# Writing a group's exponentials earlier in the instruction order of a fused convolution and two-layer MLP kernel

## The chip, the core and the metric

The kernel runs on one core of a Trainium2 chip. The core has engines that work side by side, each through its own queue in strict order: TensorE (PE in the profile; its weight loads are PEld), VectorE (DVE), ScalarE (ACT), GpSimd (POOL) and SyncE (SP), which starts the DMA transfers here. The metric is device time in microseconds (us); lower is better.

## The reference, cut to what matters

```python
w = np.exp(weight_gen - max(weight_gen)) ; w = w / (sum(w) + 1e-9)   # softmax over 7 taps
...
out = np.einsum('bshk,bskhg->bshg', w, x_unf)     # causal convolution, own weights at each position
...
rms = np.sqrt(np.mean(x * x) + 1e-6) ; xn = x / rms * rms_g          # layer 1
g = xn @ w_gate ; val = xn @ w_val ; x = (silu(g) * val) @ w_out     # 192 -> 1536 -> 192
...
h = x @ w_in ; out = (h * sigmoid(1.702 * h)) @ w_out                # layer 2: 192 -> 2048 -> 192
```

There are 8192 tokens of 192 channels; each position has 8 heads of 7 taps. All of it is float32.

## The kernel before, in words

The tokens are cut into 16 blocks of 512. Each block b goes through these steps:

- **Softmax weights**, for a group of blocks at once (GROUPS: block 0, block 1, blocks 2-3, then 4-6, 7-9, 10-12, 13-15). VectorE takes maxima (L175) and subtracts (L178): the part called pre. ScalarE takes the exponentials in one instruction (L185): ex. VectorE sums (L188), adds 1e-9 and inverts (L191, L192) and multiplies (L195): post. The tile is wraw.
- **Convolution** (conv_ops) on VectorE: seven multiplications (L226, into acc or xr) and six additions (L259), then the squares for the rms on ScalarE (L269), the power -1/2 on GpSimd (L274, L276) and the scaling (L280). A transposition and DMAs turn the block, and ScalarE and VectorE split it into a high and a low part (L319 xh, xsh; L320 xl, xsl).
- **Layer 1** in 12 units (1, b, m). TensorE forms pg and pv in PSUM, ScalarE takes silu of pg (L460, p), VectorE multiplies by pv (L464, p), ScalarE casts (L465, h), VectorE takes the remainder (L468, l). Two units later TensorE multiplies h and l by the output weights, into a and b.
- **Y**: the sums a and b of layer 1 become the input of layer 2 (L512 to L518; yh, yl, ysh, ysl).
- **Layer 2** in 8 units (2, b, i), each with two tiles ph, silu written twice by ScalarE (L481 h, L482 p) and two remainders on VectorE (L488 l), which TensorE needs one or two units later. **Z** (L530 to L538) writes the block out.

The PSUM tiles pg, pv and ph share four buffers, so a unit can start only when the tiles of two units before have been read. A pair of matmuls on the two row halves is issued together. When a PSUM bank passes from one half to the other, TensorE waits for a word that GpSimd passes on (L390); these words stand in GpSimd's queue in program order.

The units are written in the order 4 units of block b+1 (m = 0 to 3), 8 units of layer 2 of block b, then units 4 to 11 of layer 1 of block b+1, and so on. Work on the convolution of the next block is woven in: add_work(1, end, ops) puts operations in a stream that has to be written by unit end, share sets an even pace until then, and some writes an operation whenever credit allows. The convolution of block nxt is woven in from unit (1, nxt-2, 4) on (for block 4 from (1, 2, 10)), and has to be written by unit (2, nxt-2, 6), two units ahead of xt_at[nxt], where the block is turned. For a block that opens a group (nxt = 4, 7, 10, 13), pre has to be written by unit ex_at, ex is written there, and only then do post and the convolution enter the stream, with what is left of the same time:

```python
ex_at = i + 4 if gi == 2 else pos[2, nxt - 2, 2]
add_work(1, ex_at, pr)
...
if ex_hook and i == ex_at:
    ex_hook()
    ex_hook = None
    add_work(1, xt_at[nxt] - 2, post_ops + conv_ops(nxt))
```

So these exponentials stand behind the second layer-2 unit of blocks 2, 5, 8 and 11, and the stream behind them has four units, (2, nxt-2, 2) to (2, nxt-2, 5).

Of the kernel before, what the change touches and what calls it, by code (L numbers as in the profile page):

```python
# [41 lines left out]
def gated_conv_mlp(ctx: ExitStack, tc: tile.TileContext, xp, wg, w1, wo1, w2, wo2, g, out):  # L42
# [111 lines left out]
    def softmax_load(gi):  # L154
        b0, b1 = GROUPS[gi]
        n = sum(BLOCKS[b0:b1])
        t = smw.tile([P, n * 56], F32, tag="wraw", name=f"wraw{gi}")
        nc.sync.dma_start(out=t, in_=wg[:, T0[b0] * 56:(T0[b0] + n) * 56])
        return t
# [45 lines left out]
    def load_x(*bs):  # L205
        T = sum(BLOCKS[b] for b in bs)
        t0 = T0[bs[0]]
        t = big.tile([P, (T + HALO) * D], F32, tag="x", name=f"x{bs[0]}")
        cuts = [0] + [T0[b] + BLOCKS[b] + HALO - t0 for b in bs]
        for c0, c1 in zip(cuts, cuts[1:]):  # L210
            nc.sync.dma_start(out=t[:, c0 * D:c1 * D], in_=xp[:, (t0 + c0) * D:(t0 + c1) * D])
        for b in bs:
            xch[b] = t[:, (T0[b] - t0) * D:]
# [82 lines left out]
    def shuffle_x(b):  # L296

        T = BLOCKS[b]
        N = T * P
        xr = xrow.pop(b)  # L300
        h, l, sh, sl = (xtp.tile([P, NM], F32R, tag=tag, name=f"{tag}{b}") for tag in ("xh", "xl", "xsh", "xsl"))
        xT[b] = (h, l, sh, sl)
        raw = squares[0].tile([P, T * D], F32, tag="raw", name=f"raw{b}")
        nc.vector.transpose(out=raw.rearrange("p (c j t) -> p j c t", j=T, t=Q),
                            in_=xr[:, :, 0:D].rearrange("p j (c t) -> p j c t", t=Q))
        raw = raw.rearrange("p (c n) -> p c n", n=T * Q)
        full = P // Q
        for q in range(full):
            rows = slice(q * Q, (q + 1) * Q)
            cols = slice(q * T * Q, (q + 1) * T * Q)  # L310
            for c in range(D // Q):
                dst = l if c < full else sl
                for at in ((c,) if c < full else (c - full, c - full + 2)):
                    nc.sync.dma_start(out=dst.bitcast(F32)[at * Q:(at + 1) * Q, cols], in_=raw[rows, c])

        def split():
            for c, (h_, l_) in enumerate(((h, l), (sh, sl))):
                v = l_.bitcast(F32)[:, :N]
                nc.scalar.activation(out=h_[:, :N], in_=v, func=AF.Identity, scale=gt[:, c:c + 1])  # L319
                nc.vector.scalar_tensor_tensor(out=l_[:, :N], in0=v, scalar=gt[:, c:c + 1],  # L320
                                               in1=h_[:, :N].bitcast(F32), op0=ALU.mult, op1=ALU.subtract)
        return split
# [106 lines left out]
    def matmuls(ups, downs, soon=False):  # L429

        ds = [down_halves(*d) for d in downs]
        if not ups:
            (ah, al), (bh, bl) = downs_of(ds, 0, UPPER, True), downs_of(ds, 1, UPPER, False)
            (Bh, Bl), (Ah, Al) = downs_of(ds, 1, LOWER, True), downs_of(ds, 0, LOWER, False)
            upper, lower = ah + al + bh + bl, Bh + Bl + Ah + Al
        elif len(ds) < 2 or soon:
            ua, ub, lb, la = up_halves(*ups)(True)
            (ah, al), (bh, bl) = downs_of(ds, 0, UPPER, True), downs_of(ds, 1, UPPER, False)
            (Bh, Bl), (Ah, Al) = downs_of(ds, 1, LOWER, True), downs_of(ds, 0, LOWER, False)
            upper = ua + ah + al + ub + bh + bl  # L440
            lower = lb + Bh + (la + Bl if len(ds) > 1 else Bl + la) + Ah + Al
        else:
            ua, ub, lb, la = up_halves(*ups)(False)
            (ah, al), (bh, bl) = downs_of(ds, 0, UPPER, False), downs_of(ds, 1, UPPER, True)
            (Bh, Bl), (Ah, Al) = downs_of(ds, 1, LOWER, False), downs_of(ds, 0, LOWER, True)
            upper, lower = ub + bh + ua + bl + ah + al, la + Ah + Al + lb + Bh + Bl
        for f, g in zip(upper, lower, strict=True):
            f()
            g()
# [104 lines left out]
    pos = {u: i for i, u in enumerate(units)}  # L554
# [48 lines left out]
    def add_work(k, end, ops):  # L603
        streams[k].extend((end, c, f) for c, f in ops)

    def run_work(upto):
        for q in streams:
            while q and q[0][0] <= upto:
                q.popleft()[2]()

    def share(k, i):

        total, rate = 0.0, 0.0
        for end, c, _ in streams[k]:
            total += c
            rate = max(rate, total / max(1.0, at[min(end, len(units))] - at[i]))
        return rate * (at[i + 1] - at[i])

    def some(amounts):
        for k, a in enumerate(amounts):  # L620
            credit[k] += a
        while True:
            ready = [k for k in (0, 1) if streams[k] and credit[k] > 0]
            if not ready:
                return
            for k in ready:
                q = streams[k]
                spent = 0.0
                while q and credit[k] > 0 and spent < 1500:
                    _, c, f = q.popleft()  # L630
                    f()
                    credit[k] -= c
                    spent += c
# [3 lines left out]
    with ExitStack() as order:  # L637
# [42 lines left out]
        nxt = 1  # L680
        ex_hook = None
        start_at = None
        for i, u in enumerate(units):
            kind, b, m = u
            if (kind, b, m) == (1, 2, 0):
                early.close()
                late = ctx.enter_context(tc.tile_pool(name="late", bufs=6))
                parts.append((late, late))
                squares.append(ctx.enter_context(tc.tile_pool(name="squares", bufs=1)))
            run_work(i)  # L690
            late = [splits.pop(i)] if i in splits else []
            if i in xt_by_pos:
                if 2 < nxt < NB - 1:
                    load_x(nxt + 1)
                if nxt > 3:
                    splits[pos[1, nxt - 1, M1 - 2]] = shuffle_x(nxt)
                else:
                    split = transpose_x(nxt, nxt > 2)
                    late += [split] if nxt > 1 else []
                    if nxt == 1:  # L700
                        split()
                nxt += 1
                if nxt == 2:
                    start_at = pos[1, 1, 1]
                elif nxt < NB:
                    start_at = i
            if i == start_at:
                if nxt < 4:
                    load_x(nxt)
                end = xt_at[nxt]  # L710
                gi = group_of.get(nxt)
                if gi is not None and gi >= 2:
                    pr, ex_hook, post_ops = softmax_ops(gi, sm[gi])
                    ex_at = i + 4 if gi == 2 else pos[2, nxt - 2, 2]
                    add_work(1, ex_at, pr)
                else:
                    add_work(1, end - 2, conv_ops(nxt))
                gi = group_of.get(nxt + 1)
                if gi is not None and gi >= 2:
                    sm[gi] = softmax_load(gi)  # L720
# [4 lines that stand above are left out]
            downs, after = [], []  # L725
            while pend and pend[0][0] <= i:
                _, D_, key = pend.popleft()
                d, f = D_(*key)
                downs.append(d)
                after += [f] if f else []  # L730
            second, third = (U1 if kind == 1 else U2)(b, m, lambda *ups: matmuls(ups, downs, kind == 2 and b < 2))
            todo = [share(k, i) / 2 for k in (0, 1)]
            some(todo)
            second()
            some(todo)
            third()
            for f in late + after:
                f()
            if kind == 1:
                pend.append((i + 2, D1, (b, m)))  # L740
            else:

                last = len(units) - 1
                pend.append((i + 2 if b > 1 and m == 0 else i + 1, D2, (b, 2 * m)))
                pend.append((i + 1 if b < 2 or i + 1 == last else i + 2, D2, (b, 2 * m + 1)))
# [55 lines left out]
```

## Time and profile before

| | |
|---|---|
| time, median of 3 runs | 1274.84 us (1274.59 to 1278.19) |
| the profiled execution | 1278.1 us, span 1276.3 us |
| granted TensorE clock, mean | 0.991 |
| busy share: PE, DVE, ACT, POOL | 96%, 61%, 51%, 3% |

The span runs from the first to the last instruction in the trace. The busy shares are means over stages; a clock of 1 means 2.4 GHz, 0.5 means 1.2 GHz.

### The profile page before, as it was taken

To read this page: it belongs to the slowest core of one execution; us is meant where nothing else is said; L and a number is where in the kernel's file an instruction comes from. 1 tells how busy PE (TensorE), PEld (TensorE's weight loads), DVE (VectorE), ACT (ScalarE), POOL (GpSimd) and SP (SyncE) were. 2 spreads that over 40 slices of the span, in tenths; PEclk is the share of its full clock that TensorE was granted. 3 is DMA by queue.
4 is the path that set the end of the run, shared out by engine and by line. 5 is a ranking of instruction groups with operands and counts; after the bars stand their busy time and mean duration, and the time that the engine had idled before them with its cause. 6 is when DMAs were issued, how large, how long until landed. Compare 5 with 4: busy or idle time off the path is not lost.

```text
span 1276.3 us, 26762 instructions
## 1 busy us (share of the span) xinstructions
PE 1227.6 (96%) x10308; PEld 1149.5 (90%) x10308; DVE 782.8 (61%) x1294; ACT 652.7 (51%) x1273; POOL 32.4 (3%) x53
## 2 busy tenths in 40 slices
PE   6898999989999999999999999999998999999998
PEld 3676899979999887999999989998997999999997
DVE  8888957575646457574755666465467746545432
ACT  3565764554555545454454544546464454544553
POOL 4000000000000000000000000000000000000000
PEclk8899999999999999999999999999999999999999
DMA  5755511000101110110101010010001011000000
GB/s 195 232 178 160 161 38 69 2 32 16 46 9 34 33 30 1 44 41 13 37 32 30 1 41 22 32 41 32 18 14 36 26 32 30 1 13 18 2 14 13
DMA packets 35391, 58.03 MB, mean 45 GB/s; under 512 B 8256, under 2 KB 20928, under 8 KB 35264
## 3 DMA queue, kind: packets, MB, share of 16 engines
q1 hardware_dynamic: 35264, 56.33, 14.3%
q8 instruction: 81, 1.33, 0.4%
q14 instruction: 46, 0.38, 0.1%
HBM read 43.71 MB, written 6.29 MB: 39 GB/s over the span
## 4 chain that ended last, share of the span: by engine, by line
PE 83%; DVE 10%; ACT 4%; issue 3%; DMA 0%; POOL 0%; POOLq 0%; DVEq 0%
PE a L375 22%; PE ph L375 18%; PE pg L375 15%; PE b L375 14%; PE pv L375 14%; DVE xr L226 2%; DVE l L488 1%; DVE l L468 1%; DVE p L464 1%; DVE dec_a L104 1%; DVE acc L259 1%; ACT h L481 1%; DVE dec_s L108 1%; DVE dec_s L98 1%; ACT p L482 1%
## 5 line engine op out<-in xcount | busy, mean ns | idle before, releaser
L375 PE MATMUL a<-h,o 64*128 64x512 f32 x1792 | 520.9, 393 | 0.4 <-POOLq L390 0.2
L375 PEld LDWEIGHTS a<-h,o 64*128 64x128 f32 x1792 | 329.5, 185 | 9.0 <-POOLq L390 1.1
L375 PE MATMUL a<-l,o 64*128 64x512 f32 x896 | 313.6, 394 | 10.1 <-DVE l L488 9.9
L375 PE MATMUL b<-h,o 64*128 64x512 f32 x896 | 311.2, 393 | 8.0 <-POOLq L390 8.0
L375 PE MATMUL b<-l,o 64*128 64x512 f32 x896 | 311.6, 393 | 0.3 <-DVE l L468 0.3
L488 DVE TENSOR_TENSOR l<-p,h 128x512 fp32r<-128x512 f32 x256 | 175.8, 689 | 197.8 <-ACT p L482 196.6
L481 ACT ACTIVATE h<-ph 128x512 fp32r<-128x512 f32 x256 | 153.6, 600 | 226.8 <-PE ph L375 222.3
L375 PE MATMUL pv<-xh,w 64*128 64x512 f32 x768 | 242.6, 395 | 6.9 <-DVE p L464 6.6
L375 PE MATMUL pg<-xh,w 64*128 64x512 f32 x768 | 243.6, 395 | 1.3 <-ACT w L119 1.3
L375 PE MATMUL ph<-yh,w 64*128 64x512 f32 x1024 | 240.8, 393 | 0.0
L465 ACT CAST h<-p 128x512 fp32r<-128x512 f32 x192 | 119.2, 621 | 180.4 <-DVE p L464 180.4
L460 ACT ACTIVATE p<-pg 128x512 f32<-128x512 f32 x192 | 114.5, 597 | 182.0 <-PE pg L375 160.1
L464 DVE TENSOR_TENSOR p<-p,pv 128x512 f32<-128x512 f32 x192 | 131.5, 685 | 122.9 <-PE a L375 101.7
L468 DVE TENSOR_TENSOR l<-p,h 128x512 fp32r<-128x512 f32 x192 | 132.6, 691 | 97.1 <-ACT h L465 97.1
L375 PEld LDWEIGHTS a<-l,o 64*128 64x128 f32 x896 | 165.8, 185 | 20.4 <-DVE l L488 15.1
L375 PEld LDWEIGHTS b<-h,o 64*128 64x128 f32 x896 | 164.5, 185 | 14.3 <-POOLq L390 9.7
L375 PEld LDWEIGHTS b<-l,o 64*128 64x128 f32 x896 | 165.7, 185 | 5.0 <-DVE l L468 0.7
L375 PEld LDWEIGHTS ph<-yh,w 64*128 64x128 f32 x1024 | 149.6, 185 | 9.8 <-POOLq L390 0.2
L375 PE MATMUL ph<-yl,w 64*128 64x512 f32 x512 | 156.7, 392 | 0.0
L375 PEld LDWEIGHTS pv<-xh,w 64*128 64x128 f32 x768 | 141.0, 185 | 15.1 <-DVE p L464 9.6
L482 ACT ACTIVATE p<-ph 128x512 f32<-128x512 f32 x256 | 153.1, 598 | 0.9 <-DVE l L488 0.9
L375 PE MATMUL pv<-xl,w 64*128 64x512 f32 x384 | 150.5, 392 | 0.0
(106 smaller groups left out, 2114.6 us busy)
## 6 DMA issues: line engine op xcount, KB each, us to landing
x<-in_xp SPq DMA_DIRECT2D x15, 960.0 KB, 4.7
st<-in_w SPq DMA_DIRECT2D x20, 384.0 KB, 3.9
zt<-in_w SPq DMA_DIRECT2D x20, 384.0 KB, 3.5
st<-in_wo SPq DMA_DIRECT2D x14, 384.0 KB, 4.1
zt<-in_wo SPq DMA_DIRECT2D x14, 384.0 KB, 3.4
out_z<-za SPq DMA_DIRECT2D x16, 256.0 KB, 2.2
xl<-raw SPq DMA_DIRECT2D x192, 16.0 KB, 1.8
xsl<-raw SPq DMA_DIRECT2D x192, 16.0 KB, 1.8
```

The source lines that it names most:

```text
L98: nc.vector.tensor_scalar(out=t["s"], in0=hi, scalar1=-0x80000000, scalar2=4, op0=ALU.bitwise_and, op1=ALU.bitwise_or)
L104: nc.vector.scalar_tensor_tensor(out=ai, in0=ai, scalar=3, in1=t["s"], op0=ALU.logical_shift_left, op1=ALU.bitwise_or)
L108: nc.vector.tensor_single_scalar(t["s"], t["a"].bitcast(I32), -0x800000, op=ALU.bitwise_and)
L226: eng.tensor_tensor(out=dst.rearrange("p (q g) -> p q g", g=GRP), in0=x[:, (k + j0) * D:(k + j1) * D].rearrange("p (q g) -> p q g", g=GRP) ...
L375: ins = nc.tensor.matmul(ps[:, :N], w[rows], x[rows, :N], start=start, stop=stop)
L460: nc.scalar.activation(out=p[:, :N], in_=pg[:, :N], func=AF.Silu)
L464: nc.vector.tensor_tensor(out=p[:, :N], in0=p[:, :N], in1=pv[:, :N], op=ALU.mult)
L465: nc.scalar.copy(h[:, :N], p[:, :N])
L468: nc.vector.tensor_tensor(out=l[:, :N], in0=p[:, :N], in1=h[:, :N].bitcast(F32), op=ALU.subtract)
L481: nc.scalar.activation(out=h[:, :N], in_=ps[j][:, :N], func=AF.Silu, scale=SIG)
L482: nc.scalar.activation(out=p[:, :N], in_=ps[j][:, :N], func=AF.Silu, scale=SIG)
L488: nc.vector.tensor_tensor(out=l[:, :N], in0=p[:, :N], in1=h[:, :N].bitcast(F32), op=ALU.subtract)
```

## The change

The four groups that open at blocks 4, 7, 10 and 13 get the rule that the group of blocks 2-3 has already.

```diff
@@ -711,7 +711,7 @@
                 if gi is not None and gi >= 2:
                     pr, ex_hook, post_ops = softmax_ops(gi, sm[gi])
-                    ex_at = i + 4 if gi == 2 else pos[2, nxt - 2, 2]
+                    ex_at = i + 4
                     add_work(1, ex_at, pr)
```

The exponentials then stand ahead of unit (1, 5, 8) where they stood ahead of (2, 5, 2), 10 units earlier (likewise in blocks 8 and 11); in block 2 they move from (2, 2, 2) to (1, 3, 2), 4 units earlier.

ScalarE's queue around the exponentials of the group of blocks 7 to 9, before; in p_5_4 and the like the numbers are block and hidden tile, and the last number is a running one:

```order
L481 ACTIVATE h_5_3_6894<-ph_3_6853 128x512
L482 ACTIVATE p_5_3_6893<-ph_3_6853 128x512
L185 ACT_TABLE_LOAD
L185 ACTIVATE wraw_5184<-wraw_5184 128x672
L481 ACT_TABLE_LOAD
L481 ACTIVATE h_5_4_6963<-ph_4_6908 128x512
L482 ACTIVATE p_5_4_6962<-ph_4_6908 128x512
```

The same place in the change:

```order
L460 ACTIVATE p_5_7_6436<-pg_7_6400 128x512
L465 CAST h_5_7_6437<-p_5_7_6436 128x512
L185 ACT_TABLE_LOAD
L185 ACTIVATE wraw_5184<-wraw_5184 128x672
L460 ACT_TABLE_LOAD
L460 ACTIVATE p_5_8_6486<-pg_8_6450 128x512
L465 CAST h_5_8_6487<-p_5_8_6486 128x512
```

The two table loads and the exponentials have moved from between two layer-2 units to between the cast of unit (1, 5, 7) and the silu of unit (1, 5, 8).

VectorE's queue in layer 2 of block 5, from the remainder of hidden tile 5 on, before (acc and xr are the convolution of block 7):

```order
L488 TENSOR_TENSOR l_5_5_6969<-p_5_5_6967,h_5_5_6968 128x512
L259 TENSOR_TENSOR acc_6903<-acc_6903,xr_6902 128x768
L226 TENSOR_TENSOR xr_6902<-x_6210,wraw_5184 128x768
L259 TENSOR_TENSOR acc_6903<-acc_6903,xr_6902 128x768
L488 TENSOR_TENSOR l_5_6_7032<-p_5_6_7030,h_5_6_7031 128x512
L226 TENSOR_TENSOR xr_6902<-x_6210,wraw_5184 128x768
L259 TENSOR_TENSOR acc_6903<-acc_6903,xr_6902 128x768
L488 TENSOR_TENSOR l_5_7_7037<-p_5_7_7035,h_5_7_7036 128x512
L226 TENSOR_TENSOR xr_6902<-x_6210,wraw_5184 128x768
L259 TENSOR_TENSOR acc_6903<-acc_6903,xr_6902 128x768
L226 TENSOR_TENSOR xr_6902<-x_6210,wraw_5184 128x768
L488 TENSOR_TENSOR l_5_8_7095<-p_5_8_7093,h_5_8_7094 128x512
```

Layer 2 of block 5 in the change, from its first remainder on:

```order
L488 TENSOR_TENSOR l_5_0_6863<-p_5_0_6861,h_5_0_6862 128x512
L488 TENSOR_TENSOR l_5_1_6868<-p_5_1_6866,h_5_1_6867 128x512
L259 TENSOR_TENSOR acc_6447<-acc_6447,xr_6446 128x768
L488 TENSOR_TENSOR l_5_2_6912<-p_5_2_6910,h_5_2_6911 128x512
L226 TENSOR_TENSOR xr_6446<-x_6210,wraw_5184 128x768
L488 TENSOR_TENSOR l_5_3_6917<-p_5_3_6915,h_5_3_6916 128x512
L259 TENSOR_TENSOR acc_6447<-acc_6447,xr_6446 128x768
L488 TENSOR_TENSOR l_5_4_6982<-p_5_4_6980,h_5_4_6981 128x512
L226 TENSOR_TENSOR xr_6446<-x_6210,wraw_5184 128x768
L488 TENSOR_TENSOR l_5_5_6987<-p_5_5_6985,h_5_5_6986 128x512
L488 TENSOR_TENSOR l_5_6_7042<-p_5_6_7040,h_5_6_7041 128x512
L259 TENSOR_TENSOR acc_6447<-acc_6447,xr_6446 128x768
```

Between two remainders l there mostly stood two or three convolution operations, and now there is one at most; six operations of the convolution are left for layer 2, where all 13 stood.

VectorE's queue right behind the exponentials, in the change (wraw and mx are post's operations, acc the first multiplication of the convolution):

```order
L464 TENSOR_TENSOR p_5_8_6486<-p_5_8_6486,pv_8_6451 128x512
L191 TENSOR_SCALAR mx_6250<-mx_6250 128x64
L192 RECIPROCAL mx_6250<-mx_6250 128x64
L468 TENSOR_TENSOR l_5_8_6488<-p_5_8_6486,h_5_8_6487 128x512
L195 TENSOR_TENSOR wraw_5184<-wraw_5184,mx_6250 128x448
L464 TENSOR_TENSOR p_5_9_6532<-p_5_9_6532,pv_9_6497 128x512
L188 TENSOR_REDUCE mx_6250<-wraw_5184 128x32
L191 TENSOR_SCALAR mx_6250<-mx_6250 128x32
L192 RECIPROCAL mx_6250<-mx_6250 128x32
L468 TENSOR_TENSOR l_5_9_6534<-p_5_9_6532,h_5_9_6533 128x512
L195 TENSOR_TENSOR wraw_5184<-wraw_5184,mx_6250 128x224
L226 TENSOR_TENSOR acc_6447<-x_6210,wraw_5184 128x768
```

In the change post lies among the products p and remainders l of layer 1; one operation of it, the sum L188 of the first part, stands ahead of the first of these rows. Behind them follow p and l of unit 10, the split of the next block (xl, xsl), a multiplication of the convolution and p of unit 11. In block 2 the exponentials stand behind the four ScalarE operations of Y and ahead of the silu of unit (1, 3, 2).

## Rows read from the trace of the kernel before

**Rows 1.** The page's first line.

```profile
span 1276.3 us, 26762 instructions
```

**Rows 2.** Windows from Y to Z of blocks 2, 3, 5, 8 and 11.

```profile
core 0: us, PE busy (x) PEld busy (x) DVE busy (x) ACT busy (x) POOL busy (x), PEclk, DMA share, GB/s
248.24:305.07 56.83, 52.97 (x424) 47.13 (x423) 37.38 (x58) 29.55 (x56) 1.20 (x2) 0.94 0.07 21
330.60:379.65 49.05, 49.05 (x425) 47.35 (x424) 26.62 (x40) 25.53 (x53) 1.20 (x2) 1.00 0.08 24
479.45:533.67 54.22, 50.25 (x425) 43.89 (x424) 37.39 (x58) 29.47 (x56) 1.20 (x2) 1.00 0.07 22
708.15:762.49 54.34, 50.24 (x425) 47.38 (x423) 37.41 (x58) 29.51 (x57) 1.20 (x2) 1.00 0.07 23
936.87:991.04 54.17, 50.16 (x424) 47.45 (x423) 37.40 (x58) 29.49 (x56) 1.20 (x2) 1.00 0.08 23
```

**Rows 3.** ScalarE's timeline, block 5: start, duration, instruction, [idle before it].

```profile
492.54 1.28 ACT L185 ACT_TABLE_LOAD   x1
493.83 0.77 ACT L185 ACTIVATE wraw<-wraw 128x672 f32<-128x672 f32 x1
...
495.91 0.60 ACT L481 ACTIVATE h<-ph 128x512 fp32r<-128x512 f32 x1
```

**Rows 4.** TensorE's timeline: two waits of block 5, the last of block 2.

```profile
504.32 0.50 PE L375 MATMUL a<-l,o 64*128 64x512 f32 x1 [1.13 <-DVE l L488]
...
515.49 0.49 PE L375 MATMUL b<-h,o 64*128 64x512 f32 x1 [1.74 <-POOLq L390]
...
284.17 0.79 PE L375 MATMUL b<-h,o 64*128 64x512 f32 x1 [2.66 <-POOLq L390]
```

**Rows 5.** GpSimd's timeline, block 5.

```profile
515.19 0.19 POOL L274 TENSOR_SCALAR ss<-ss 128x4 f32<-128x4 f32 x1 [79.60 <-ACT xr L269]
```

**Rows 6.** Windows behind the last wait of block 2; columns as in rows 2.

```profile
284.00:288.00 4.00, 3.83 (x18) 3.68 (x20) 1.61 (x5) 0.01 (x1) 1.06 (x2) 0.50 0.19 79
288.00:292.00 4.00, 4.00 (x29) 3.80 (x28) 1.39 (x2) 2.16 (x4) 0.00 (x0) 0.72 0.00 0
```

**Rows 7.** ScalarE's timeline, layer 1 of block 5, and the split of block 6.

```profile
459.28 0.62 ACT L465 CAST h<-p 128x512 fp32r<-128x512 f32 x1 [0.75 <-DVE p L464]
461.19 0.60 ACT L460 ACTIVATE p<-pg 128x512 f32<-128x512 f32 x1 [1.28 <-PE pg L375]
...
469.57 0.72 ACT L319 ACTIVATE xh<-xl,gt 128x512 fp32r<-128x512 f32 x1
```

**Rows 8.** VectorE's timeline, the same stretch.

```profile
461.82 0.69 DVE L464 TENSOR_TENSOR p<-p,pv 128x512 f32<-128x512 f32 x1 [1.19 <-PE a L375]
...
468.32 0.69 DVE L464 TENSOR_TENSOR p<-p,pv 128x512 f32<-128x512 f32 x1 [0.65 <-PE a L375]
...
470.32 0.75 DVE L320 SCALAR_TENSOR_TENSOR xl<-xl,gt,xh 128x512 fp32r<-128x512 f32 x1
```

**Rows 9.** TensorE's timeline: first matmuls of two units and of xl.

```profile
464.87 0.39 PE L375 MATMUL pg<-xh,w 64*128 64x512 f32 x1
...
471.38 0.39 PE L375 MATMUL pg<-xh,w 64*128 64x512 f32 x1
...
471.84 0.39 PE L375 MATMUL pg<-xl,w 64*128 64x512 f32 x1
```

**Rows 10.** VectorE's timeline, block 2: post's first operation, the operation behind post.

```profile
263.36 0.62 DVE L188 TENSOR_REDUCE mx<-wraw 128x64 f32<-128x448 f32 x1 [1.39 <-ACT wraw L185]
...
267.12 0.95 DVE L226 TENSOR_TENSOR acc<-x,wraw 128x768 f32<-128x768 f32 x1
```

**Rows 11.** Block 2 behind Y: the timelines of ScalarE, VectorE and TensorE.

```profile
250.69 0.59 ACT L460 ACTIVATE p<-pg 128x512 f32<-128x512 f32 x1
...
251.43 0.68 DVE L464 TENSOR_TENSOR p<-p,pv 128x512 f32<-128x512 f32 x1
...
253.14 0.67 PE L375 MATMUL ph<-yh,w 64*128 64x512 f32 x4
```

## What the change does to the time: the prediction

> **What bounds the kernel now.** I looked first at where blocks differ. The four blocks in whose layer 2 exponentials are written are 2, 5, 8 and 11, and windows from Y to Z set them beside a block without: block 3 takes 49.05 us with TensorE busy in all of it, and the four take 56.83, 54.22, 54.34 and 54.17 [rows 2]. So TensorE is the bound, a block whose matmuls never wait needs 49.05, and the four lose 7.78, 5.17, 5.29 and 5.12 us, together 23.36 us of a span of 1276.3 [rows 1]. VectorE is busy for 37.4 us of these stretches, against 26.6 in block 3.
>
> Next, the waits of TensorE inside such a stretch. ScalarE is held by the exponentials from 492.54 to 495.91 [rows 3], but TensorE's first wait behind them that is longer than 0.5 us ends at 504.32, 8 us later, and it is for a remainder l of VectorE (1.13 us; a second one like it follows 6 us on) [rows 4]. This is VectorE's queue: post and all 13 convolution operations stand among the remainders of four units, which are too short for them, so that l comes late. The last wait, 1.74 us at 515.49 in block 5 and 2.66 us at 284.17 in block 2, is for GpSimd's queue [rows 4], and there stands the reason too: the rms instruction starts at 515.19, released by the squares on ScalarE [rows 5], which had waited for the late convolution; the word for TensorE's bank stands behind it. In block 2 that wait is long enough that the granted clock falls behind it, to 0.50 and then 0.72 in the next two windows of 4 us (0.50 is 1.2 GHz, 1 is 2.4) [rows 6]; so its loss is 2.6 us larger than the 5.2 of the others. What wait ends last in these stretches is thus always the crowded convolution, not the exponentials.
>
> **The change, part by part.** No instruction is added or removed: at each of the four places two table loads and one activation move, pre is drawn together and post and the convolution spread out. No DMA moves past another in SyncE's queue.
>
> *The gain in layer 2.* The stream behind the exponentials has 14 units in blocks 5, 8 and 11 where it had 4, and 8 units in block 2. Six convolution operations are left for layer 2 in block 5, one at most between two remainders. A remainder's duration of 0.69 and an operation's of 0.95 (VectorE's longest) [rows 8, 10] make 2 x 0.69 + 2 x 0.95 = 3.3 us per layer-2 unit, and the units are about 4.4 us long (estimate: 19 pairs of matmuls that start 0.23 us apart; in [rows 9] two pairs lie between 471.38 and 471.84). So l is in time, the squares come before GpSimd has to wait for them, and I take each stretch down to block 3's 49.05: -23.36 us. More is excluded, since TensorE has no idle time in block 3; nothing at all is the other bound.
>
> *The price in layer 1, blocks 5, 8 and 11.* ScalarE's three instructions hold it for 495.91 - 492.54 = 3.37 us [rows 3]. In unit (1, 5, 7) the cast ends at 459.28 + 0.62 = 459.90, and the silu of unit 8 starts at 461.19 after 1.28 us of idle time [rows 7]. With the exponentials between, it starts at 459.90 + 3.37 = 463.27, 2.08 late; the product p of unit 8 at 461.82 + 2.08 = 463.90 [rows 8], done at 464.59. Unit 10 takes over its PSUM buffers at 464.87 [rows 9]: 0.28 us to spare, no wait. VectorE then has post in the way, 3.07 us in all (from 263.36 to 267.12, less the 0.69 of an l that lies between) [rows 8, 10]. From the start of the product p of unit 8 to that of unit 10 its queue holds, as the change orders it, two products and two remainders (4 x 0.69), post without its first sum (3.07 - 0.62 = 2.45) and the first convolution operation (0.95). Run through without a pause these are 6.16 us: p of unit 10 starts at 470.06, against 468.32 [rows 8, 10], 1.74 late. (They overlap a little at their ends, and l waits a little for its cast; I set the one against the other.) The split of block 6 stands behind it. It starts at 469.57 + 1.74 = 471.31 and gives xh 0.72 later, at 472.03, and xl at 470.32 + 1.74 + 0.75 = 472.81 [rows 7, 8]. TensorE wants xh at 471.38 and xl 0.46 later [rows 9]. It waits 0.65 for xh and 0.32 more for xl: 1.0 us per block, 3.0 for three. Behind that the buffers are free in time, and the convolution runs at a pace much like block 3's. The cover is thin: bounds are nothing, and the 2.08 by which ScalarE is late.
>
> *The price in block 2.* The exponentials stand behind Y, where ScalarE is late already. The silu of unit (1, 3, 2) moves from 250.69, and its product from 251.43, by 3.37, to 254.80; the product is done at 255.49, and TensorE wants its buffers for the first layer-2 unit at 253.14 [rows 11]. That is a wait of 2.35 us. The convolution then has fewer units than in block 5, and a remainder may be late once: I add 0.6, half of the 1.13 that such a wait took [rows 4], with bounds of 0 and 1.13. Together 2.9.
>
> *Sum:* -23.36 + 3.0 + 2.9 = -17.5 us. The profiled execution took 1278.1 us (span 1276.3), at the top of the three runs; the terms are differences between stretches of it and carry over to the median: 1274.84 - 17.5 = 1257.3.
>
> *A rule against it.* In the three instructions the exponentials start at 493.83, 0.01 us after the end of the 1.28 us table load [rows 3]. The Trainium skill (ScalarE: Activation LUTs, "What ACT_TABLE_LOAD costs") puts a switch of tables at 1.28 us for the load, which this trace agrees with, and 1.38 us more for draining the engine, which it doesn't show. By that page ScalarE would be held some 2.8 us longer at each place, and the gain would shrink by about 11 us, to an estimated 6.5.
>
> **The rivals.** Changes below 0.3% (3.8 us) can't be told from none here.
>
> (A) The move is hidden: slack in layer 1 covers the exponentials everywhere. Then -23.4: 1251.5. For it: 1.28 us of ScalarE's idle time per unit, and the 0.28 us of reserve at unit 10 [rows 7, 9]. Against it: the silu in block 2 has no idle time ahead of it [rows 11]. 0.17.
>
> (B) Nothing is hidden: TensorE stops for all of ScalarE's 3.37 us at the four places, because VectorE, with post, an l and p per unit and the convolution, never catches up in layer 1. Then -23.4 + 13.5 = -9.9: 1264.9. For it: p of unit 10 is still 1.7 late. Against it: units have up to 1.2 us of idle time on VectorE [rows 8]. 0.14.
>
> (C) The change does not do what it does on paper: the 5 us belong to the exponentials wherever they stand (3.37 and what follows from a late ScalarE), and move with them: 1274.8. The place of the waits, 8 to 20 us behind the exponentials, and their releasers speak against it [rows 4, 5]. 0.05.
>
> (D) Slower. The place is the first matmul behind the delayed product. If TensorE's stop there is long enough for the clock to fall, as behind the last wait of block 2 [rows 6], one place costs what block 2 costs now, 7.78: four cost 31.1, and -23.4 + 31.1 = +7.8 gives 1282.6. It decides from 23.36 / 4 = 5.84 us per place. Against it: waits of 1.1 to 1.7 us in block 5 left the clock at 1.00 [rows 2, 4], and the longest that I get is 2.35. 0.04.
>
> (E) ScalarE is held longer than the rows add up to: a pause as long as the load (1.28) behind each of the eight loads, 10.2 us, all of it in TensorE's way: -7.3, 1267.5. Only the rule above speaks for it, the 0.01 us against it [rows 3]. 0.02.
>
> **How the numbers follow.** The forecast, a gain between 15 and 20 us (1254.8 to 1259.8), has 0.58. Predicted: 1257.3. The range takes in (A) and (B), which are the bounds of the prices, with half a microsecond of scatter at the lower end: 1251 to 1265. (E), (C) and (D), 0.11 together, are left out. Faster by over 0.3%: 0.58 + 0.17 + 0.14 + 0.02 = 0.91; within 0.3%, (C): 0.05; slower, (D): 0.04.
>
> **What would show it right or wrong.** In the changed profile Y to Z of blocks 5, 8 and 11 takes 49.0 to 49.5 us, that of block 2 about 52, with a clock of 1.00 in all four; the waits for l (L488) and for GpSimd's queue in those stretches are gone; TensorE waits once per group for xh or xl, some 1.0 us, and once for p (L464) in front of block 2's layer 2, 2.3 us; the rms instruction on GpSimd is no longer released by the squares. I am wrong if waits for l remain in layer 2 (the pace was not the cause), if the stretch from Z to the next Y grows by over 2 us in blocks 5, 8 and 11 (the price is larger), or if TensorE's clock falls there.

## The result, and the profile after

The change takes 1261.19 us (median of 5 runs, 1260.78 to 1261.96) against 1277.18 for the kernel before (5 runs, 1274.59 to 1278.62): a ratio of 0.988, 95% interval 0.986 to 0.990. The forecast was 1257.3 with a range of 1251 to 1265. The profiled execution has a span of 1260.1 us, 16.2 less than before. The kernel before runs at two levels of time, about 1275 and about 1278 us (e8 to e10 below), and 1277.18 lies at the upper one; over all 24 executions of it on record the median is 1275.4, and against that the change gains 14.2 us.

Windows from Y to Z of blocks 2, 5, 8 and 11 of the changed kernel, with the columns of [rows 2]:

```profile
249.50:302.51 53.01, 51.30 (x425) 47.42 (x423) 36.44 (x56) 29.36 (x57) 1.20 (x2) 0.97 0.07 23
477.73:526.78 49.05, 49.05 (x425) 48.49 (x423) 29.17 (x44) 25.92 (x54) 1.20 (x2) 1.00 0.08 25
701.93:750.90 48.97, 48.97 (x424) 44.05 (x423) 29.14 (x44) 25.68 (x53) 1.21 (x2) 1.00 0.08 25
925.95:974.94 48.99, 48.99 (x424) 48.53 (x423) 29.15 (x44) 25.91 (x53) 1.20 (x2) 1.00 0.08 25
```

Blocks 5, 8 and 11 are at the length of a block without exponentials, 49.0, with TensorE busy throughout: 15.7 us less than the sum in [rows 2]. Block 2 is 3.8 shorter than in that execution, but stays 4.0 above the others, and its clock is 0.97. The waits for l and for GpSimd's queue are gone from all four. The rms instruction shows it for GpSimd's queue; the end of the squares on ScalarE and the rms on GpSimd in the changed kernel, block 5:

```profile
505.20 0.19 ACT L269 ACTIVATION_READ_ACCUMULATOR xr<-acc 128x1 f32 x1
...
506.97 0.19 POOL L274 TENSOR_SCALAR ss<-ss 128x4 f32<-128x4 f32 x1 [73.99 <-ACT h L481]
```

In [rows 5] the squares on ScalarE released it, so that the words behind it stood still; now they end at 505.39, 1.6 us ahead of it, and it is released by layer 2's own work.

The price lies between Z and the next Y. The stretches that hold the exponentials now, in the changed kernel:

```profile
451.52:477.73 26.21, 26.04 (x223) 25.11 (x221) 19.68 (x37) 14.53 (x22) 0.00 (x0) 1.00 0.11 30
675.74:701.93 26.19, 26.04 (x221) 25.05 (x220) 19.67 (x37) 14.54 (x22) 0.00 (x0) 1.00 0.11 30
899.67:925.95 26.28, 26.22 (x223) 22.64 (x221) 19.69 (x37) 14.64 (x22) 0.00 (x0) 1.00 0.11 29
```

The same stretches of the kernel before:

```profile
454.05:479.45 25.40, 25.40 (x222) 22.17 (x220) 13.03 (x23) 11.58 (x19) 0.00 (x0) 1.00 0.11 31
682.64:708.15 25.51, 25.51 (x222) 25.51 (x221) 13.02 (x23) 11.58 (x19) 0.00 (x0) 1.00 0.11 30
911.45:936.87 25.42, 25.42 (x222) 25.42 (x220) 13.04 (x23) 11.59 (x20) 0.00 (x0) 1.00 0.11 30
```

They are 0.81, 0.68 and 0.86 us longer, 2.35 together (forecast 3.0). The place is the one foretold. ScalarE's timeline of the changed kernel in block 5, from the cast of unit 7 to the silu of unit 8, and the split:

```profile
456.76 0.62 ACT L465 CAST h<-p 128x512 fp32r<-128x512 f32 x1 [0.76 <-DVE p L464]
457.40 1.28 ACT L185 ACT_TABLE_LOAD   x1
458.69 0.77 ACT L185 ACTIVATE wraw<-wraw 128x672 f32<-128x672 f32 x1
459.48 1.28 ACT L460 ACT_TABLE_LOAD   x1
460.77 0.60 ACT L460 ACTIVATE p<-pg 128x512 f32<-128x512 f32 x1
...
468.38 0.72 ACT L319 ACTIVATE xh<-xl,gt 128x512 fp32r<-128x512 f32 x1
```

and TensorE's, where the unit that reads xh begins:

```profile
468.64 0.39 PE L375 MATMUL a<-l,o 64*128 64x512 f32 x1
469.15 0.49 PE L375 MATMUL pg<-xh,w 64*128 64x512 f32 x1
...
469.94 0.50 PE L375 MATMUL pg<-xl,w 64*128 64x512 f32 x1
```

The three instructions take 460.77 - 457.40 = 3.37 us as before, without a pause at the switches. xh ends at 469.10, and the first matmul on it starts 0.51 us behind the last of the unit ahead, where 0.23 is the step; xl comes 0.79 later instead of 0.46. These two gaps, 0.28 and 0.33, are 0.6 of the 0.8 us; TensorE shows no other gap over 0.1 us in this stretch, and where the rest lies is not shown.

In block 2 the stop at the first layer-2 unit is there as well. TensorE's timeline of the changed kernel:

```profile
256.10 0.49 PE L375 MATMUL ph<-yh,w 64*128 64x512 f32 x1 [1.48 <-ACT p L460]
256.82 0.73 PE L375 MATMUL ph<-yh,w 64*128 64x512 f32 x3 [0.23 <-DVE p L464]
```

and windows of 4 us around it:

```profile
252.00:256.00 4.00, 2.62 (x23) 2.18 (x19) 2.08 (x5) 3.94 (x5) 0.00 (x0) 1.00 0.00 0
256.00:260.00 4.00, 3.67 (x21) 2.74 (x23) 3.85 (x9) 1.43 (x4) 0.00 (x0) 0.75 0.00 0
260.00:264.00 4.00, 4.00 (x32) 3.24 (x30) 3.96 (x6) 2.42 (x5) 0.00 (x0) 0.82 0.00 0
```

The gaps beyond the step of 0.23 are 1.65 and 0.49, a stop of 2.1 us (forecast 2.35). But behind it the clock is at its lower level for a part of each of the two windows (0.75 and 0.82): matmul pairs start some 0.43 us apart up to 261. The remaining 1.8 of the 4.0 us I put down to that, and the forecast had a clock of 1.00 there.

By these windows the two traces differ by 15.7 + 3.8 - 2.35 = 17.2 us, and their spans by 16.2. Z of block 1, ahead of which the two kernels are the same, comes 207.0 us into the span of the changed kernel and 205.9 into that of the kernel before: 1.2 us that are no part of the change.

### The profile page after: what moved, and what is told of

Its sections match the earlier page's. It is cut to its first block, busy times and chain, and to the rows that moved or that the text cites. A ratio compares the mean times of both kernels' runs of the same rounds, so it can differ in the third digit from the quotient of the medians.

```text
span 1260.1 us, 26761 instructions
## 1 busy us (share of the span) xinstructions
PE 1224.0 (97%) x10308; PEld 1143.1 (91%) x10308; DVE 779.2 (62%) x1294; ACT 651.3 (52%) x1273; POOL 32.5 (3%) x53
## 4 chain that ended last, share of the span: by engine, by line
PE 88%; DVE 8%; ACT 2%; issue 1%; DMA 0%; DVEq 0%; ACTq 0%; POOLq 0%
PE a L375 24%; PE ph L375 21%; PE b L375 15%; PE pv L375 15%; PE pg L375 14%; DVE p L464 1%; DVE l L468 1%; DVE dec_a L104 1%; DVE xr L226 1%; DVE dec_s L108 1%; DVE dec_s L98 1%; ACT h L465 0%; DVE zt L100 0%; ACT L460 0%; DVE acc L259 0%
## 5 line engine op out<-in xcount | busy, mean ns | idle before, releaser
L375 PEld LDWEIGHTS pv<-xh,w 64*128 64x128 f32 x768 | 140.8, 185 | 15.6 <-DVE p L464 9.7
```

The source lines that it names most:

```text
L375: ins = nc.tensor.matmul(ps[:, :N], w[rows], x[rows, :N], start=start, stop=stop)
```

## The experiments

**The exponentials early, the convolution late (e1).** This parts the two things that the change moves at once. ex stays at i + 4; post and the convolution enter the stream at the old place.

```diff
...
                 ex_hook = None
-                add_work(1, xt_at[nxt] - 2, post_ops + conv_ops(nxt))
+                go_at = pos[2, nxt - 2, 2] if nxt > 2 else i
+            if i == go_at:
+                add_work(1, xt_at[nxt] - 2, post_ops + conv_ops(nxt))
...
```

> The exponentials stand where the change puts them, but post and the convolution enter the stream only where they did before, at unit (2, nxt-2, 2). If the crowded convolution is what cost 5 us per block (theory), Y to Z of blocks 5, 8 and 11 goes back to about 54 us and that of block 2 to 55 to 58, with the waits for l and for GpSimd's queue, while Z to Y of blocks 5, 8, 11 falls from 26.2 to about 25.5: some 1275 to 1279 us. If the exponentials cost it wherever they delay layer 2 (rival), Y to Z stays at 49 to 50 and the time near 1261.

It took 1279.11 us, 1.003 of before (1.002 to 1.004): the whole gain is gone, with the exponentials where the change has them. The window from Y to Z of block 5 in e1, and TensorE's waits in it (total, times, longest):

```profile
482.22:536.52 54.30, 51.46 (x424) 46.30 (x423) 36.71 (x56) 26.17 (x53) 1.20 (x2) 0.97 0.07 22
PE b L375 <- POOLq L390: 1.7, 1, 1.7
PE a L375 <- DVE l L488: 1.1, 1, 1.1
```

54.30 us, 54.38 and 54.61 in blocks 8 and 11, though ScalarE loads no table there. Z to Y fell to 25.4 and 25.5. In block 2 both costs add up, 58.23, a little above what was expected, and so is the time. The rival falls: crowding brings the loss back without the exponentials.

It doesn't bring back all of the waits. In block 5 the kernel before waits for l twice (2.2 us together; the first stands in [rows 4]); here the first of the two is gone, in blocks 8 and 11 too. Counted as gaps beyond the step of 0.23, TensorE's stops in block 5 are 3.3 us here and 4.7 in the kernel before. What fills the stretch up to 54 again is the clock, which falls behind the wait for GpSimd's queue in all three blocks (in block 5, 0.71 and 0.86 from 516 to 520 and from 520 to 524 us), as it doesn't there in the kernel before. So the crowding is the larger part of the stops; 1.2 to 1.4 us per block go when the exponentials (and the part of pre that stood ahead of them) leave layer 2, since post and the convolution can't start before them.

**A second exponential at the old place (e2).** The counterpart: the change, with an exponential and its two table loads in layer 2 again, a smaller one than before.

```diff
+            if b in (2, 5, 8, 11) and (kind, m) == (2, 2):
+                spare = squares[0].tile([P, P], F32, tag="spare", name=f"spare{b}")
+                nc.scalar.activation(out=spare, in_=ident, func=AF.Exp)
```

> The change, and at the old place, ahead of (2, b, 2) of blocks 2, 5, 8 and 11, a second exponential of a 128x128 tile into a tile that nobody reads, with its two table loads: some 2.9 us more of ScalarE there. Theory: layer 2 has the slack for it when the convolution is spread out, Y to Z of blocks 5, 8 and 11 stays at 49 to 50, the time within 3 us of 1261. Rival (the exponentials themselves were the cost there): Y to Z of about 54, 1276 to 1281 us.

1261.25 us, 0.989 of before (0.988 to 0.991), no different from the change. Block 5 in e2, from Y to Z:

```profile
476.62:525.68 49.06, 49.06 (x425) 47.80 (x423) 29.16 (x44) 28.51 (x57) 1.20 (x2) 1.00 0.08 25
```

ScalarE is busy for 2.6 us more than in the change (the exponentials moved take 3.37), and TensorE doesn't wait at all. Two table loads in layer 2 cost nothing here, where VectorE is on time.

**Block 2 at its old place (e3).**

```diff
-                    ex_at = i + 4
+                    ex_at = pos[2, 2, 2] if nxt == 4 else i + 4
```

> The change without block 2, whose exponentials stay at (2, 2, 2). Theory: Y to Z of block 2 goes back to 56.8 us with a clock of 0.94, the other three stay at 49.0, the time is 3.8 us longer: 1265. If the gain in block 2 was a matter of this one execution, the time stays at 1261.

1261.88 us (1260.76 to 1262.98), 0.989 of before (0.988 to 0.991). That is a miss: it is 0.7 us longer than the change and not 3.8. In its trace block 2 shows the waits of the kernel before, and not its clock (window from Y to Z, then TensorE's waits):

```profile
247.78:301.90 54.12, 50.21 (x424) 43.69 (x424) 37.38 (x58) 29.55 (x57) 1.20 (x2) 1.00 0.07 22
PE b L375 <- POOLq L390: 2.7, 1, 2.7
PE a L375 <- DVE l L488: 1.1, 1, 1.1
```

So 2.7 of the 7.78 us that I read from [rows 2] as block 2's loss were the low clock, which this execution doesn't have.

**The kernel before, three times more (e8, e9, e10).** No edit. The question is whether the clock behind that wait is low in some executions only.

> The kernel before once more, for its trace. If the low clock behind the last wait of block 2 is there in some executions only, Y to Z of block 2 takes 54.1 us with a clock of 1.00 here, as in e3, and the execution is near 1275; if it belongs to the kernel, 56.8 and 0.94.

> The kernel before, another execution. Theory: the time of an execution and block 2's clock go together: near 1275 us with Y to Z of block 2 in 54.1 us at a clock of 1.00, or near 1278 with 56.8 at 0.94. Rival (the two levels of time come from the start of the kernel): 56.8 and 0.94 at 1275 too.

> As e9, one more execution, since one alone may fall on the same level again.

They took 1278.18, 1277.48 and 1274.94 us. Y to Z of block 2 and the window behind its last wait, in e8:

```profile
248.23:305.10 56.87, 53.00 (x424) 47.69 (x423) 37.38 (x58) 29.59 (x56) 1.20 (x2) 0.94 0.06 21
284.00:288.00 4.00, 3.80 (x18) 3.69 (x20) 1.61 (x5) 0.00 (x0) 1.10 (x2) 0.50 0.17 71
```

in e9:

```profile
249.05:304.45 55.40, 51.44 (x424) 48.18 (x423) 37.38 (x58) 29.50 (x56) 1.20 (x2) 0.97 0.07 22
284.00:288.00 4.00, 3.02 (x14) 2.93 (x16) 1.61 (x5) 0.60 (x4) 1.20 (x2) 0.57 0.36 152
```

in e10:

```profile
248.25:302.40 54.15, 50.16 (x424) 47.40 (x423) 37.39 (x58) 29.61 (x56) 1.20 (x2) 1.00 0.07 22
284.00:288.00 4.00, 3.81 (x32) 3.81 (x34) 2.13 (x6) 1.64 (x4) 1.09 (x2) 1.00 0.17 69
```

The wait is 2.7 us in all of them, and the block takes 56.87, 55.40 or 54.15 us with what the clock does behind it. e8 alone came out as if the low clock belonged to the kernel, and e9 lies between its two expectations; e10 shows that it does not. The times of the executions follow in order: of the 3.2 us between the spans of e8 and e10, 2.7 are block 2. Of the 2.5 between e9 and e10, 1.25 are block 2 and 0.8 lie ahead of Z of block 1, so that the rival (the start) has a part there. Of the 24 executions of the kernel before, 17 lie between 1274.6 and 1276.5 us, and seven between 1277.2 and 1280.0. That the seven are those with a low clock in block 2 is shown only for the three of them that have a trace.

**Post and the convolution behind the split (e4).** The price in blocks 5, 8 and 11: is it post in VectorE's queue, or the late silu itself?

```diff
...
                 ex_hook = None
-                add_work(1, xt_at[nxt] - 2, post_ops + conv_ops(nxt))
+                go_at = i + 3 if nxt > 4 else i
+            if i == go_at:
+                add_work(1, xt_at[nxt] - 2, post_ops + conv_ops(nxt))
...
```

> The change, but for blocks 7, 10 and 13 post and the convolution enter the stream three units behind the exponentials, behind the split of the next block. Theory (post in VectorE's queue makes xh and xl late): Z to Y of blocks 5, 8 and 11 falls from 26.2 to about 25.5 us, Y to Z stays at 49.0 to 49.5, the time is about 2 us shorter, 1259. Rival (the late silu behind the table loads is the price): Z to Y stays at 26.2 and the time at 1261.

1259.53 us, 0.988 of before (0.986 to 0.989). Z to Y and Y to Z of block 5 in e4:

```profile
450.48:475.88 25.40, 25.40 (x222) 25.40 (x221) 17.22 (x34) 14.83 (x23) 0.00 (x0) 1.00 0.11 31
475.88:524.87 48.99, 48.99 (x424) 45.93 (x423) 31.47 (x47) 25.55 (x54) 1.20 (x2) 1.00 0.08 25
```

25.40 us, and 25.49 in blocks 8 and 11; TensorE is busy in all of it, and the 11 units that are left carry the convolution. The late silu is hidden, as the reserve of 0.28 us said (e1's 25.4 and 25.5 show it too), and the price was what stands ahead of the split in VectorE's queue: post and the first operation of the convolution, which e4 moves together. The time fell by 1.7 us from the change's, near the 2.3 of the stretches.

**Block 2 at three other places (e5, e6, e7).** All three are e4 with another number: the exponentials of block 2 stand 2, 1 or 6 units behind i.

```diff
-                    ex_at = i + 4
+                    ex_at = i + (2 if nxt == 4 else 4)
```

> As e4, and in block 2 the exponentials two units earlier, ahead of Y and of the silu of unit (1, 3, 0). Theory: the 4 us that block 2 still loses are a stop of 2.1 us at the first layer-2 unit, because the exponentials stand behind Y, and the low clock behind that stop; ahead of Y the stop is under 1 us and the clock stays at 1.00. From Z of block 1 to Z of block 2 takes 95.5 us in e4 and should take 92 to 93: about 3 us less than e4, 1256 to 1257. Rival (the loss is the shorter stream of the convolution, not the place): no change, 1259.5.

> As e4, and in block 2 the exponentials three units earlier, right behind the split of block 3, where ScalarE has no idle time left. Theory (the place decides, not the length of the stream): TensorE stops again, 1.5 to 3 us, so that this is slower than e5 by 1 to 3 us although the convolution has a unit more: 1257 to 1260. Rival (longer stream is better): as fast as e5 or faster.

> As e4, and in block 2 the exponentials two units later, ahead of the first layer-2 unit. Theory: the stop behind Y goes, and the clock with it, but the convolution has six units left and waits for l or for GpSimd's queue come back, 1 to 3 us: Z of block 1 to Z of block 2 in 93 to 95 us, 1257.5 to 1259.5. Rival (the convolution's pace is no matter in block 2): 92 us, 1256.

From Z of block 1 to Z of block 2 they take 93.63, 94.78 and 95.10 us (e4: 95.47; e10: 96.50), and the kernels 1257.03 (0.984 of before, 0.982 to 0.987), 1258.47 (0.985, 0.983 to 0.988) and 1258.58 (0.985, 0.983 to 0.988). In e5 the clock is 1.00 in each window of 4 us around its one long wait, here the one that holds it:

```profile
252.00:256.00 4.00, 2.80 (x24) 1.96 (x22) 3.24 (x6) 2.13 (x5) 0.00 (x0) 1.00 0.00 0
PE ph L375 <- DVE p L464: 1.2, 1, 1.2
```

That is a stop of 1.5 us at the first layer-2 unit, where I had expected under 1, and 0.4 at a unit ahead of it; 93.63 is thus above the 92 to 93 expected. In e6 there are two stops, one in layer 1 right behind the split, and one at the first layer-2 unit again; TensorE's timeline of e6:

```profile
244.78 0.50 PE L375 MATMUL pg<-xh,w 64*128 64x512 f32 x1 [0.93 <-ACT p L460]
245.50 0.50 PE L375 MATMUL pv<-xh,w 64*128 64x512 f32 x1 [0.22 <-DVE p L464]
...
256.74 0.73 PE L375 MATMUL ph<-yh,w 64*128 64x512 f32 x3 [0.88 <-DVE p L464]
```

The matmul ahead of the first started at 243.46, so that 1.1 and 0.5 us are lost there; the one ahead of the last started at 255.47, and 1.0 us is lost. The clock is 1.00. Behind the first layer-2 unit TensorE waits for nothing in e5 and in e6, so that a longer stream has nothing to buy there. In e7 the stop behind Y is gone (0.2 us is left), and TensorE's waits from Y to Z are those of a crowded convolution again, only smaller:

```profile
PE b L375 <- POOLq L390: 1.2, 1, 1.2
PE a L375 <- DVE l L488: 1.0, 1, 1.0
PE ph L375 <- ACT p L482: 0.2, 1, 0.2
```

So in block 2 place and length both count, and two units behind i is the best of the four: e5 beats the change by some 4 us and the kernel before by 18.

## Why the prediction was right, and by how much it was off

*What bounds it.* The crowded convolution as the cause of the loss in layer 2 is shown from both sides: e1 brings the loss back without the exponentials there, e2 brings an exponential back without the loss. The prediction's "not the exponentials" goes a little too far: without them e1 lacks the first of the two waits for l. The wait for GpSimd's word comes and goes with the pace. That the rms holds up the word is read from the order in time (the rms at 515.19, the matmul at 515.49 [rows 4, 5]); no run takes the rms out of that queue.

*The gain in layer 2, blocks 5, 8, 11.* Foretold 15.6 us, measured 15.7.

*The price there.* Foretold 3.0, measured 2.35, at the split as foretold. VectorE's timeline of the changed kernel, p of units 8 and 10:

```profile
461.41 0.69 DVE L464 TENSOR_TENSOR p<-p,pv 128x512 f32<-128x512 f32 x1 [1.29 <-ACT p L460]
...
467.13 0.68 DVE L464 TENSOR_TENSOR p<-p,pv 128x512 f32<-128x512 f32 x1
```

From one to the other VectorE took 467.13 - 461.41 = 5.72 us, and not 6.16: its operations overlap at their ends by more than they wait. So xh was 0.28 late where 0.65 was foretold, and xl the 0.33 more that was foretold. e4 takes the price away by moving post and the convolution behind the split.

*Block 2* is the term that was mis-sized, on both sides. Its gain went in with 7.78 us, of which 2.7 was the low clock of the one execution profiled; e10 loses 54.15 - 49.0 = 5.1 there. The sentence that failed is that the terms "are differences between stretches of it and carry over to the median": this one doesn't, since that median, 1274.84, lies at the time of e10 (1274.94), which has the clock at 1.00 there. And the price went in with 2.9 us, 2.35 for the stop and 0.6 for a late remainder; the stop was 2.1, no remainder was late, and 1.8 came from the clock behind the stop. That is rival (D)'s mechanism, at one of the four places, and one of the signs of being wrong that the prediction names (a clock that falls) came true in block 2. What spoke against (D), that waits of 1.1 to 1.7 us left the clock at 1.00, did not carry as far as a stop of 2.1, and in e1 the clock fell behind waits of 1.7 to 2.0.

Put right, the sum is 15.7 + (54.15 - 53.01) - 2.35 = 14.5 us, and 1274.94 (e10) - 14.5 = 1260.4, against 1261.19 measured. So nearly all of the gain is in the three later groups; block 2's move alone is worth about 1 us (from Z of block 1 to Z of block 2, 96.50 in e3 and 95.47 in the change; 0.7 between their times).

*How near it came.* 1261.19 lies in the range, but above the 1254.8 to 1259.8 that had the largest chance, and 3.9 above the forecast. The gain of 16.0 against 1277.18 falls between the 15 and 20 us foretold; that is luck, as three of these five executions of the kernel before lie at its upper level. Against 1275.4, the median of all, it is 14.2.

*The rivals.* (A), all hidden, did not come; e4 shows what it takes in blocks 5, 8 and 11, and in block 2 no run hides it all (e5 still stops for 1.9 us). (B) fell: ScalarE's 3.37 us are hidden in layer 1 but for 0.8. (C) fell by e1 and e2. (E) fell: in the changed kernel too the three instructions follow each other within 0.02 us. The 1.38 us of draining that the Trainium skill (ScalarE: Activation LUTs, "What ACT_TABLE_LOAD costs") adds to each switch does not show in this trace.

## What to carry to other kernels

When one engine's work has to be done by a deadline, the operation that opens it (here a single activation) belongs early enough that the rest can be spread out; look for the loss not at that operation but, as here, 8 to 20 us behind it, where queues that it has nothing to do with stand still. When operations are moved up, look at what stands behind them in each queue up to the next deadline: here post and the convolution did better behind the split of the next block than ahead of it. And a stretch with a clock below 1 should be priced with and without the clock, since the next execution may not have it.

## What the runs showed of the hardware that was not expected

The clock behind one and the same wait is not the same in each execution: behind 2.7 us of waiting it was 0.50 and 0.72 in two windows of 4 us (e8), 0.57 and 1.00 (e9), 1.00 and 1.00 (e10, e3). Behind the stop of 2.1 us in block 2 of the change, it fell in each of the traces with it (the change, e2, e4: Y to Z in 53.01 to 53.03 us, at a mean of 0.97; and e1). Behind the wait for GpSimd's queue in blocks 5, 8 and 11, 1.7 to 2.0 us long, it fell in all three blocks of e1; in the four traces of the kernel before, where that wait is 1.7 to 1.9 us, it fell in none. Behind the shorter stops of e5, e6 and e7 it stayed at 1.00. The length of a stop alone thus doesn't decide it; what does is open. In the change the 1.8 us of low clock were nearly as much as the stop itself.
